# Row statistics of the second token pair taken in the first pair's chunks and kept, and all due times set anew, in a two-layer attention and SwiGLU kernel

## The chip, the cores and the metric

The kernel runs on one core of a Trainium2 chip. The metric is the device time of one execution in microseconds (us). A core has five engines that run side by side: TensorE (PE in the profile, with PEld for its weight loads), VectorE (DVE), ScalarE (ACT), GpSimd (POOL) and SyncE (SP), which here issues nearly all DMAs. Each engine takes its own instructions strictly in the order in which they were written into the program, and waits on semaphores where an instruction needs another engine's result.

## What is computed

Two layers, each of which is an attention block A and a feed-forward block B on x of 2048 tokens by 512 features, in float32. Both layers share the weights.

```python
x = x + A(layernorm(x)); x = x + B(layernorm(x))      # layer 0
x = x + A(layernorm(x)); x = x + B(layernorm(x))      # layer 1

def layernorm(x):
    m = mean(x, axis=-1); v = var(x, axis=-1)
    return (x - m) / sqrt(v + 1e-5)

def A(x):                          # 32 heads of 16, 4 segments of 512 tokens, one after the other
    for each segment s:
        p = softmax(q_s k_s^T / 4 + causal mask);  a_dot = p v_s
        a_mem = (phi(q_s) M) / (phi(q_s) z + 1e-6)
        o_s = g * a_mem + (1 - g) * a_dot
        M += phi(k_s)^T v_s;  z += sum(phi(k_s))
    return o @ wo

def B(x):                          # 512 -> 1792 -> 512
    return (silu(x @ w_gate) * (x @ w_up)) @ w_down
```

## The kernel before

**Precision.** A float32 operand is split into a high part of type float32r and the rest, also float32r; a product is made of three TensorE passes (high by high, rest by high, high by rest). So every weight and every activation that goes into a matmul is first copied by ACT (the high part) and then subtracted by DVE or POOL (the rest).

**Attention.** There are 32 units for a layer: 4 segments by 4 groups of 8 heads by 2 halves. Of each unit there are projections (`qk_proj`, `v_proj`, through `mm3`, line 295), row maxima (`mx_units`, lines 558 and 564), scores, exponentials and products with v (`at_units`, lines 609 to 636), the memory (`mem_read`, `mem_update`) and, a segment later, `wo_proj`. A segment's rows are loaded and normalised in `ln_pre` and transposed in `ln_fin`. Each projection's result goes through DRAM (`scrq`, `scrk`) and comes back as `cq` and `ck`.

**Feed-forward.** The tokens are taken in four blocks of 512, as two pairs: blocks 0 and 1 (m = 0), then 2 and 3 (m = 1). The 1792 hidden features are taken in seven chunks of 256. Chunk 0 of a pair is computed plainly (`up`, line 1019). Chunks 1 to 6 use Strassen's scheme with 7 products instead of 8 on the halves of the 2x2 block matrix (`strassen`, lines 1049, 1062, 1064). For them `make_t` (lines 963, 984, 985) builds the sums and differences of a pair's transposed rows on DVE, 28 DVE operations a pair, and `load_s` (lines 902 to 916) those of the weights on POOL. `finish` (lines 1003 to 1006) multiplies gate and up and splits the product; `down` (lines 1093, 1098) multiplies a chunk with w_down and adds it to the rows of the block, and with the last chunk stores them. The opening of the feed-forward part is interleaved with the last units of attention by `hook` and `EARLY_AT`.

**Normalising in the feed-forward part.** `ln(b)` loads each of a block's four tiles of 128 rows from `xmid` into `xin` (two buffers, in turn), and calls `ln_norm`: `bn_stats` (line 367) and `bn_aggr` (368) on DVE, the addition of epsilon (369) and the power of -1/2 (370) on POOL, the product of mean and scale on DVE (372), and the normalising itself on POOL (379) into `xn` (two buffers, in turn). `ln_transpose` brings the tile onto TensorE (387), and ACT (391) and DVE (392) copy and split it.

**What sets the order.** The program is written as a list of operations, each with an engine, a planned cost, what it reads and writes, and a due time, `P.prio`. `at(v)` sets the due time to `base + v * T`, with T = 15.0 in attention and 16.7 in the feed-forward part. `Program.issue` is a list scheduler: it goes through time with the planned costs, and on each engine takes among the operations that are ready the one with the smallest due time; an engine never idles in the plan while something is ready. The resulting order of each engine is what is written into the program. So a due time decides only between operations that are ready together, and buffers (which are reused in program order) hold operations back besides. The due times come from tables: `OFF` (attention, one row for each layer: `at` scores, `mx` maxima, `lf` transposes, `lp` normalising, `mr`/`mu` memory, `wo`, `qk`, `qe`, `v` projections), `PRE` (start of a layer: `w1` to `w3`, `lv`, `lo` weight loads, `gate` the gate, `c` and `mb` clearings, `v`, `dv`, `qk1` projections), `EP` (opening of the feed-forward part) and the constants `PAIR` (between the pairs), `STEP` (between the chunks), `TAT` (`make_t`, for each pair), `WAT` (the first `load_s`), `FIN` (`finish`) and `WQ1`. A planned cost on POOL is the first argument of `gp`.

The lines that set the due times of the feed-forward loop, in the form before:

```python
v = m * PAIR                          # the pair
...
at(v + WAT);     load_s(1, "g")
at(v + TAT[m]);  make_t(m)
...
v = m * PAIR + 2 + (c - 1) * STEP     # chunk c = 1..6
at(v);           gs = strassen(c, "g", m)
...
at(v + FIN);     finish(...)
```

## Time and profile before

| what | value |
|---|---|
| median of 3 runs | 1877.89 us (1874.88 to 1881.86) |
| the profiled execution | 1875.12 us |
| its span, first to last instruction | 1873.4 us |
| mean granted TensorE clock | 0.996 |
| instructions | 33021 |

All views below are of that one execution. In the rows of stages the columns are: from and to in us, length, then for PE, PEld, DVE, ACT and POOL the busy time with the number of instructions, and last the mean granted TensorE clock, the mean busy share of the DMA engines and GB/s. In the rows of groups stand line, engine, operation, what it writes and reads, the shapes and the number of instructions, then busy time and mean duration in ns, then the idle time before them and what ended it. In the rows of waits stand the waiting engine, tile and line, what it waited for, the total in us, the number of waits and the longest. In the rows of the timeline stand start and length in us; a wait before the instruction stands in brackets with what ended it. A name such as `s` or `ps` stands for all buffers of that kind.

### The profile page before, as it was taken

The numbers are of one execution on the slowest core, as the hardware profiler recorded it, in microseconds if no ns is written. First come the engines' busy times: TensorE is split into PE (matmuls) and PEld (weight loads), VectorE is DVE, ScalarE is ACT, GpSimd is POOL, SyncE is SP. The second block draws the span as 40 slices with busy tenths as digits, with TensorE's granted clock in tenths as the row PEclk, the third lists the DMA queues.
The fourth block names the chain that finished last, engine by engine and source line by source line (L and its number), as shares of the span: only waits on it lengthen the run. The fifth ranks groups of instructions, "written<-read, shape, count | busy, mean of one in ns | idle before, by whom it ended". The sixth has DMA issues, their size and how long they took to land.

```text
span 1873.4 us, 33021 instructions
## 1 busy us (share of the span) xinstructions
PE 1823.4 (97%) x11360; PEld 1449.7 (77%) x11360; DVE 1406.8 (75%) x3834; ACT 872.0 (47%) x1629; POOL 916.9 (49%) x1184
## 2 busy tenths in 40 slices
PE   7999999999999999999989999999999999999999
PEld 5787787777778887788777777788777778878887
DVE  6878788788876678765776777787898766795656
ACT  4565564555533433333435655556454433333432
POOL 6344444444656554646533444444445647444551
PEclk9999999999999999999999999999999999999999
DMA  8435444464232132212363353455542311221111
GB/s 243 142 103 146 137 130 148 145 198 132 77 120 62 46 90 85 62 45 63 118 209 103 103 162 111 136 169 138 191 121 74 124 51 57 86 78 51 44 58 45
DMA packets 126967, 206.14 MB, mean 110 GB/s; under 512 B 14160, under 2 KB 52048, under 8 KB 126800
## 3 DMA queue, kind: packets, MB, share of 16 engines
q1 hardware_dynamic: 124752, 203.49, 36.5%
q8 instruction: 91, 1.49, 0.3%
q10 hardware_dynamic: 2048, 0.53, 0.1%
q14 instruction: 76, 0.62, 0.1%
HBM read 136.34 MB, written 67.11 MB: 109 GB/s over the span
## 4 chain that ended last, share of the span: by engine, by line
PE 74%; DVE 14%; issue 5%; DMA 4%; ACT 2%; POOL 2%; SPq 1%; DVEq 0%; POOLq 0%; ACTq 0%
PE ps L1049 23%; PE ps L295 14%; PE ps L1093 13%; PE ps L558 6%; PE ps L636 6%; PE ps L609 6%; DVE junk L564 3%; PE ps L1019 2%; DMA ck<-scrk 2%; DVE tt L963 1%; DVE s L1098 1%; DVE s L985 1%; PE ps L387 1%; DMA s<-nm 1%; DVE mx L564 1%
## 5 line engine op out<-in xcount | busy, mean ns | idle before, releaser
L1049 PE MATMUL ps<-s,s 128*128 128x512 f32 x2016 | 547.2, 396 | 7.7 <-DVE s L985 4.6
L295 PE MATMUL ps<-s,s 128*128 128x512 f32 x1536 | 524.0, 406 | 4.7 <-ACT s L451 3.0
L564 DVE CUSTOM_DVE_ANT_0 junk<-ps,amask 128x128 bf16<-128x128 f32 (+3 forms) x1024 | 433.7, 484 | 48.8 <-PE ps L558 47.4
L1049 PEld LDWEIGHTS ps<-s,s 128*128 128x128 f32 x2016 | 376.4, 188 | 103.4 <-DVE s L985 5.5
L1093 PE MATMUL ps<-s,vt 128*128 128x512 f32 x1296 | 379.9, 398 | 2.2 <-ACT vt L1005 2.2
L295 PEld LDWEIGHTS ps<-s,s 128*128 128x128 f32 x1536 | 286.1, 190 | 53.2 <-issue 5.6
L615 ACT ACTIVATE s<-ps 128x512 f32<-128x512 f32 x448 | 253.8, 610 | 106.8 <-PE ps L609 95.8
L1093 PEld LDWEIGHTS ps<-s,vt 128*128 128x128 f32 x1296 | 245.8, 190 | 59.0 <-ACT vt L1005 2.6
L558 PE MATMUL ps<-ck,s 127*128 127x256 f32 (+2 forms) x1024 | 277.7, 335 | 7.2 <-DMA ck<-scrk 5.9
L609 PE MATMUL ps<-s,ck 128*128 128x256 f32 x1280 | 249.9, 287 | 4.8 <-DMA s<-nm 2.9
L609 PEld LDWEIGHTS ps<-s,ck 128*128 128x128 f32 x1280 | 220.9, 189 | 36.2 <-DVE mx L564 4.3
L1098 DVE TENSOR_TENSOR s<-s,ps 128x512 f32<-128x512 f32 x224 | 150.0, 682 | 91.6 <-PE ps L1093 91.5
L619 POOL TENSOR_SCALAR_AFFINE_SELECT s<-s 128x512 f32<-128x512 f32 x192 | 126.4, 661 | 170.2 <-ACT s L615 167.8
L558 PEld LDWEIGHTS ps<-ck,s 127*128 127x128 f32 x1024 | 178.2, 190 | 31.7 <-issue 6.0
L492 POOL TENSOR_SCALAR s<-raw 128x512 fp32r<-128x512 f32 x64 | 45.2, 706 | 177.2 <-ACT raw L491 168.8
L916 POOL TENSOR_TENSOR s<-mem,s 128x512 fp32r<-128x512 f32 x96 | 130.3, 1357 | 0.0
L1019 PE MATMUL ps<-s,s 128*128 128x512 f32 x384 | 124.0, 400 | 0.9 <-ACT s L391 0.9
L923 POOL COPY turn<-vt 128x1 f32<-128x1 f32 x20 | 3.7, 184 | 232.9 <-DVE vt L1006 232.9
L636 PE MATMUL ps<-s,vt 128*32 128x384 f32 (+3 forms) x1536 | 115.7, 419 | 0.2 <-DVE mx L564 0.2
L636 PEld LDWEIGHTS ps<-s,vt 128*32 128x32 f32 x1536 | 43.4, 109 | 64.2 <-issue 46.5
L615 ACT ACTIVATE pc<-ps 128x512 f32<-128x512 f32 x128 | 78.9, 616 | 20.5 <-PE ps L609 19.8
L1019 PEld LDWEIGHTS ps<-s,s 128*128 128x128 f32 x384 | 71.6, 188 | 19.3 <-ACT s L391 1.9
(171 smaller groups left out, 2589.0 us busy)
## 6 DMA issues: line engine op xcount, KB each, us to landing
s<-scrq SPq DMA_DIRECT2D x128, 192.0 KB, 3.5
ck<-scrk SPq DMA_DIRECT2D x128, 192.0 KB, 4.4
scrq<-s SPq DMA_DIRECT2D x32, 512.0 KB, 3.6
scrk<-s SPq DMA_DIRECT2D x32, 512.0 KB, 3.3
scrq<-s SPq DMA_DIRECT2D x32, 256.0 KB, 3.2
scrk<-s SPq DMA_DIRECT2D x32, 256.0 KB, 2.5
s<-xmid SPq DMA_DIRECT2D x32, 256.0 KB, 5.3
xin<-xmid SPq DMA_DIRECT2D x32, 256.0 KB, 2.6
```

The source lines that it names most:

```text
L295: pe(n, passes, lambda: nc.tensor.matmul(view(ps.ap), lhsT=av(a.ap), rhs=bv(b.ap), start=start, stop=stop), [(a, rk[0]), (b, rk[1])], [ps])
L558: nc.tensor.matmul(ps.ap[:, a * 256:a * 256 + nk], lhsT=cq.ap[0:127, 2 * j + p, qt * 128:(qt + 1) * 128], rhs=ck.ap[0:127, p, 0:nk], start ...
L564: dve(w, lambda a=a, qt=qt, w=w, ps=ps, junk=junks[qt % 2]: nc.vector.tensor_tensor_reduce(out=junk.ap[:, :w], in0=ps.ap[:, a * 256:a * 25 ...
L609: nc.tensor.matmul(ps.ap[:, 256 * p:256 * p + 256], lhsT=ck.ap[:, p, kt * 128:kt * 128 + 128], rhs=cq.ap.rearrange("r (j p) c -> r p j c", ...
L615: act(512, lambda: nc.scalar.activation(view().rearrange("p x i c -> p (x i c)"), ps.ap, AF.Exp, scale=SCALE), [ps], [(Pb, key)], table="exp")
L619: gp(0.593, lambda: nc.gpsimd.affine_select(out=view()[:, 0], in_=view()[:, 0], pattern=[[0, 4], [1, 128]], compare_op=OP.is_ge, fill=0.0, ...
L636: nc.tensor.matmul(ps.ap[32 * i:32 * i + 32, qt * 128:(qt + k) * 128], lhsT=vt.ap[:, kt, VW * hd:VW * hd + 32], rhs=view(k=k)[:, :, idx], ...
L916: gp(n / 400, lambda hi=hi, lo=lo, src=src: nc.gpsimd.tensor_sub(lo(), src(), hi().bitcast(F32)), [read, (wt, (o0, 0))], [(wt, (o0, 1))])
L1019: pe(512, 1, lambda i=i, j=j, kc=kc, x=x, ps=ps, wt=wt: nc.tensor.matmul(ps.ap, lhsT=wt.ap[:, i, kc, cs], rhs=XT[b][j].ap[:, :, kc], start ...
L1049: pe(512, 1, lambda i=i, kc=kc, x=x, buf=buf, view=view: nc.tensor.matmul(ps.ap, lhsT=w.ap[:, o, i, kc], rhs=view(buf.ap, kc), start=(x == 0),
L1093: pe(512, 1, lambda i=i, j=j, fi=fi, x=x, ps=ps, wt=wt, cs=cs: nc.tensor.matmul(ps.ap, lhsT=ht.ap[:, 0:2048].rearrange("p (f a c) -> p f a ...
L1098: dve(512, lambda ps=ps, t=t: nc.vector.tensor_add(xb.ap[:, t, :], xb.ap[:, t, :], ps.ap), [ps, (xb, t)], [(xb, t)])
```

## The change

It has three parts.

1. `ln_norm` is taken apart: `ln_stats` holds lines 367 to 372, and `ln_norm` calls it only when it isn't handed finished statistics. A new function `stats(b)` loads the four tiles of a block and keeps their two columns of statistics in a new buffer `rsall`. It is called for block 2 in chunk 3 and for block 3 in chunk 4 of pair 0, with the due time of the chunk plus 1.0. `ln(2)` and `ln(3)` load the rows again and only normalise.
2. All due times in the tables are new.
3. The planned costs of POOL's operations are new.

```diff
+STC, STV = 3, 1.0
-PAIR, STEP, WAT, TAT = 11.852, 7.441, 15.217, (16.363, 16.627)
+PAIR, STEP, WAT, TAT = 14.368, 2.101, 18.234, (6.403, -7.127)
-FIN = 4.95
-WQ1 = -11.849
+FIN = -18.907
+WQ1 = -35.921
-OFF = ({'qe': (-8.094, 0.816), 'at': (3.287, 3.306), 'mx': (-0.131, -0.724), 'lf': (1.377, -12.744), 'mr': (-1.477, 8.495), 'mu': (-0.96, 1.713), 'wo': (1.48, 1.471), 'qk': (-3.167, 5.871), 'v': (3.082, -3.254), 'lp': (-0.438, 1.332)},
-       {'qe': (-13.863, -20.735), 'at': (1.287, 1.907), 'mx': (0.952, -1.245), 'lf': (-8.163, -17.558), 'mr': (12.428, -6.81), 'mu': (-3.524, 1.251), 'wo': (0.699, 4.133), 'qk': (2.417, 0.184), 'v': (-2.402, 1.541), 'lp': (-15.902, 3.529)})
-PRE = {'w1': -7.923, 'w2': -0.782, 'w3': 1.908, 'c': -7.288, 'mb': 12.995, 'lv': 2.037, 'lo': 1.091, 'gate': 1.265, 'v': 1.734, 'dv': 17.818, 'qk1': -29.691, 'mx': -0.352}
-EP = {'w': 7.501, 'wn': 13.81, 'ln': -3.176, 'dn': -0.03, 'up': -1.79}
+OFF = ({'qe': (-12.069, -0.112), 'at': (3.013, 4.323), 'mx': (-0.349, -1.509), 'lf': (-11.355, -18.547), 'mr': (5.356, 2.737), 'mu': (-0.143, 0.695), 'wo': (1.6, 0.626), 'qk': (-2.074, 4.084), 'v': (4.063, -4.114), 'lp': (-0.398, 0.122)},
+       {'qe': (-5.653, -33.367), 'at': (0.791, 0.725), 'mx': (0.972, -0.361), 'lf': (-24.563, -10.349), 'mr': (10.993, -6.845), 'mu': (-3.987, -0.752), 'wo': (5.165, -12.31), 'qk': (-0.437, 1.019), 'v': (-0.149, 1.562), 'lp': (-34.686, 18.305)})
+PRE = {'w1': -22.172, 'w2': 0.92, 'w3': 0.959, 'c': 10.734, 'mb': 21.744, 'lv': 1.211, 'lo': 1.157, 'gate': -12.416, 'v': 41.354, 'dv': 19.399, 'qk1': -33.145, 'mx': -6.145}
+EP = {'w': 27.342, 'wn': 3.181, 'ln': -1.549, 'dn': 3.109, 'up': -0.862}
...
-    def ln_norm(xt, view, xk, tags, on_act=False):
-        st, mv, rs = sb("bst", [128, 6], ring=4), sb("bmv", [128, 2], ring=4), sb("brs", [128, 2], ring=4)
+    def ln_stats(xt, view, xk, home=None):
+        st, mv = sb("bst", [128, 6], ring=4), sb("bmv", [128, 2], ring=4)
+        rs, i = rk = home or (sb("brs", [128, 2], ring=4), 0)
         dve(512, lambda: nc.vector.bn_stats(out=st.ap, in_=view(xt.ap)), [(xt, xk)], [st])
         dve(8, lambda: nc.vector.bn_aggr(out=mv.ap, in_=st.ap), [st], [mv])
         gp(0.18, lambda: nc.gpsimd.tensor_scalar_add(mv.ap[:, 1:2], mv.ap[:, 1:2], EPS), [mv], [mv])
...
+        return rk
+
+    def ln_norm(xt, view, xk, tags, on_act=False, rk=None):
+        rs, i = rk = rk or ln_stats(xt, view, xk)
         xn = sb(tags, [128, 512])
...
+        RS = {}
+        two_rs = sb("rsall", [128, 16])
+
+        def stats(b):
+            for t in range(4):
+                xt = sb("xin", [128, 512], ring=2)
+                load_rows(xt, x_in, b * 512 + t * 128)
+                RS[b, t] = ln_stats(xt, lambda a: a, None, (two_rs, 8 * b + 2 * t - 16))
+
         def ln(b):
...
-                ln_transpose(ln_norm(xt, lambda a: a, None, XN2), XT[b][0], XT[b][1], t)
+                ln_transpose(ln_norm(xt, lambda a: a, None, XN2, rk=RS.get((b, t))), XT[b][0], XT[b][1], t)
...
             for c in range(1, NF):
                 v = m * PAIR + 2 + (c - 1) * STEP
+                if m == 0 and c in (STC, STC + 1):
+                    at(v + STV)
+                    stats(c + 2 - STC)
                 at(v)
                 gs = strassen(c, "g", m)
```

The planned costs on POOL (us): the power in `ln_stats` 0.46 to 0.6, normalising 0.75 to 0.85, `qk_proj` 0.59 to 0.70 and 1.23 to 1.32, the mask on the exponentials 0.593 to 0.66, the rest of `of` 1.23 to 1.32, the sums in `load_s` 0.65 to 0.85, and its splits from n / 400 to 0.3 + n / 480.

30 lines of the change are left out of this document (15 added, 15 removed).

## The prediction

> **What bounds the kernel now.** I read the busy table first, then the engines by stage, then the waits of PE, and last the timeline at the places where PE waits.
>
> ```profile
> span 1873.4 us, 33021 instructions
> PE 1823.4 (97%) x11360; PEld 1449.7 (77%) x11360; DVE 1406.8 (75%) x3834; ACT 872.0 (47%) x1629; POOL 916.9 (49%) x1184
> ```
>
> PE is busy for 1823.4 of 1873.4 us. The change removes no matmul, so what it can win is mainly within the 50.0 us in which PE stands idle. The execution took 1875.1 us, 1.7 more than its span, and the median of the runs is 1877.9, another 2.8 more: I work out a difference against the profiled execution and set it on the median.
>
> Engines by stage (attention of layer 0, opening of its feed-forward part, chunks of pair 0, turn from pair 0 to pair 1, boundary of the layers, and the same in layer 1):
>
> ```profile
> 0.00:60.00 60.00, 43.63 (x199) 34.70 (x200) 40.61 (x137) 28.11 (x51) 32.03 (x55) 0.97 0.72 220
> 60.00:470.00 410.00, 404.20 (x3403) 319.69 (x3402) 326.39 (x1254) 229.94 (x455) 178.72 (x271) 1.00 0.48 142
> 470.00:545.00 75.00, 72.92 (x388) 56.08 (x387) 62.52 (x109) 33.30 (x60) 46.34 (x54) 1.00 0.36 113
> 545.00:690.00 145.00, 145.00 (x626) 116.66 (x625) 98.68 (x151) 58.58 (x102) 81.35 (x89) 1.00 0.19 54
> 690.00:770.00 80.00, 76.82 (x345) 61.08 (x343) 68.39 (x113) 28.80 (x52) 43.36 (x48) 1.00 0.31 97
> 935.00:1000.00 65.00, 58.87 (x299) 46.64 (x298) 45.71 (x159) 26.24 (x48) 22.02 (x21) 0.95 0.54 174
> 1000.00:1400.00 400.00, 392.10 (x3313) 310.50 (x3312) 313.71 (x1203) 224.86 (x442) 172.13 (x265) 1.00 0.49 141
> 1400.00:1475.00 75.00, 72.97 (x388) 56.07 (x387) 61.61 (x107) 33.37 (x60) 46.04 (x54) 1.00 0.35 112
> 1625.00:1690.00 65.00, 62.29 (x278) 49.89 (x277) 55.78 (x88) 23.58 (x44) 34.97 (x36) 0.97 0.27 86
> ```
>
> Length less PE busy gives the idle time: start 16.4, attention 5.8 and 7.9, openings 2.1 and 2.0, turns 3.2 and 2.7, boundary 6.1; in the chunks nothing. What ended it, from the waits of PE:
>
> ```profile
> PE ps L387 <- ACT xn L376: 9.9, 1, 9.9
> PE ps L558 <- DMA ck<-scrk: 5.9, 5, 2.2
> PE ps L1049 <- DVE s L985: 4.6, 2, 2.3
> PE ps L295 <- ACT s L451: 3.0, 2, 1.8
> ```
>
> The first is the ramp at the start. The third is the pair of turns: PE waits for the last split of `make_t`.
>
> **The change, part by part.** *The turn.* The statistics of a block's four tiles in the opening (470 to 545) and in the turn (690 to 735), then DVE's and PE's timeline:
>
> ```profile
> L367 DVE BATCH_NORM_STATS2 bst<-xin x8: 649/680/689, 470.7 to 500.9; 128x6 f32<-128x512 f32 x8
> ```
> ```profile
> L367 DVE BATCH_NORM_STATS2 bst<-xin x4: 655/670/685, 702.4 to 712.7; 128x6 f32<-128x512 f32 x4
> ```
> ```profile
> 706.09 0.16 DVE L372 SCALAR_TENSOR_TENSOR brs<-bmv,brs 128x1 f32<-128x1 f32 x1 [2.01 <-POOL brs L370]
> ...
> 726.58 1.28 DVE L963 TENSOR_TENSOR xn<-s 128x512 f32<-128x512 f32 x2
> ...
> 743.52 1.68 DVE L963 TENSOR_TENSOR of<-of,s 128x512 f32<-128x512 f32 x1
> ...
> 752.59 1.21 DVE L985 TENSOR_TENSOR s<-tt,s 128x512 fp32r<-128x512 f32 x1
> ```
> ```profile
> 752.73 0.50 PE L1049 MATMUL ps<-s,s 128*128 128x512 f32 x1 [2.32 <-DVE s L985]
> ```
> ```profile
> 726.58:753.80 27.22, 27.12 (x40) 1.00 0.18 57
> ```
> ```profile
> 726.60:753.80 27.20, 14.79 (x20) 1.00 0.18 57
> ```
> ```profile
> 726.60:753.80 27.20, 6.86 (x8) 1.00 0.18 57
> ```
>
> The last three rows are DVE from the first operation of `make_t` to its last: all of it, `L963` alone, `L985` alone. It is full, and `make_t` is (14.79+6.86)/28 = 0.77 us an operation. So the turn ends when DVE has done its pile, and PE pays 2.3 us. What one tile's statistics cost:
>
> ```profile
> L367 DVE BATCH_NORM_STATS2 bst<-xin 128x6 f32<-128x512 f32 x60 | 40.4, 680 | 7.5 <-DMA xin<-in_A_x_dram 6.1 <-DMA xin<-xlay 1.5
> L368 DVE BATCH_NORM_AGGREGATE bmv<-bst 128x2 f32<-128x6 f32 x64 | 10.8, 172 | 0.6
> L369 POOL TENSOR_SCALAR bmv<-bmv 128x1 f32<-128x1 f32 x64 | 17.8, 281 | 41.5 <-DVE bmv L368 39.9 <-DVE rm L694 0.9 <-DVE brs L372 0.3
> L370 POOL TENSOR_TENSOR brs<-bmv,mhalf 128x1 f32<-128x1 f32 x64 | 38.8, 609 | 3.7
> L372 DVE SCALAR_TENSOR_TENSOR brs<-bmv,brs 128x1 f32<-128x1 f32 x64 | 16.3, 255 | 18.7 <-POOL brs L370 18.4
> ```
>
> On DVE 0.68+0.17+0.26 = 1.11 us, and as a chain through POOL 2.0 us. A turn holds four tiles, those of block 3; the opening's eight are those of blocks 1 and 2, so block 2 is measured there already. By 4 x 1.11, 4.4 us leave a full DVE, and 2.0 us go between a row's landing and its normalising (at 706.09 DVE itself waits 2.0 for POOL). That is more than the 2.3 us of PE's wait. Besides, `make_t` of pair 1 gets a smaller due time (7.24 instead of 28.48 units of 16.7), so its operations go ahead of the adds of `down`. I take the two waits (4.6) and 0.4 of the small ones behind them: -5.0. Bounds: -5.9 (all idle of both turns) and 0.
>
> Waits have a second price:
>
> ```profile
> 935.00:952.00 17.00, 12.66 (x48) 9.57 (x47) 11.43 (x19) 6.44 (x10) 6.63 (x3) 0.90 0.68 204
> 952.00:962.00 10.00, 10.00 (x44) 8.38 (x45) 8.61 (x34) 1.73 (x3) 1.92 (x2) 0.83 0.65 241
> 1680.00:1690.00 10.00, 7.73 (x28) 5.90 (x27) 6.78 (x9) 2.33 (x5) 6.10 (x6) 0.83 0.27 79
> ```
>
> The granted clock is 0.83 over the 10 us around the wait of layer 1's turn, so 0.17x10 = 1.7 us more are lost; the same in each of the two boundary stretches. In layer 0's turn the clock stayed at 1.00 (row 690:770). So -1.7 for one turn; bounds 0 and -3.4. The Trainium skill ("TensorE: Matmul & The Clock Gate", What's actually happening) says that the clock halves after at least one idle window of about 3.4 us. The waits here are 2.3 us, shorter than that, and three of them are followed by a low clock: the trace differs, and the row decides; by the rule alone the clock terms would be nothing and my sum 3.4 us smaller.
>
> *The statistics in their new place.* The list scheduler starts the most urgent ready operation, and where none is ready, a less urgent one. The statistics need only rows in `xmid` and a free `xin`, so I expect them as soon as block 1's tiles are out, about 490 to 545, ahead of chunk 3. There are eight tiles in each opening instead of four: 4 x 1.11 = 4.4 us of DVE into 75 - 62.5 = 12.5 us of idle. `make_t` of pair 0 is now due at 6.40, ahead of them (7.20, 9.30), where it stood behind block 2 (16.36 against 10.65). I take 0; bounds -2.0 per opening (its idle) and +4.4 (all on the chain). If they stand in the chunks, DVE idles 46 us of 145 there.
>
> *Rows twice.* 16 more loads of 256 KB:
>
> ```profile
> xin<-xmid SPq DMA_DIRECT2D x32, 256.0 KB, 2.6
> ```
> ```profile
> SPq L860 <- POOL s L916: 115.6, 19, 15.9
> ```
>
> The DMA engines are at 0.19 to 0.36 in those stages, so bandwidth costs nothing. But SP takes its queue in order: in chunks of pair 0 it stood 115.6 of 145 us before weight loads whose `raw` POOL had not freed. A row load behind such a wait keeps `bn_stats` waiting at DVE's head, and behind it the adds that free Strassen's banks. 0 while the loads lie in the opening; one such stall could be some us.
>
> *Boundary.* The elementwise end of a chunk (`FIN`) goes from +4.95 to -18.9, ahead of everything on ACT and DVE. Now:
>
> ```profile
> 937.74 7.16 PE L1093 MATMUL ps<-s,vt 128*128 128x512 f32 x23 [2.18 <-ACT vt L1005]
> ...
> 951.91 0.48 PE L558 MATMUL ps<-ck,s 127*128 127x256 f32 x2 [2.16 <-DMA ck<-scrk]
> ```
>
> The first wait is for that end's cast. When it goes, the second comes late: the ck chain starts elsewhere. I take -1.0 net and one clock window, -1.7; bounds -9.5 (6.1 idle and two windows) and 0.
>
> *Start.* `make_gate`'s five loads move ahead of the rows of x:
>
> ```profile
> 10.23 2.45 SPq L341 DMA_DIRECT2D bet<-in_A_beta_dram  x4
> ```
>
> About 2.5 us of SP ahead of what ends the ramp of 9.9; against that, the last wq and wk loads, now behind the gate, move up, and PE waits 3.0 for `L451`. 0; bounds -3.0 and +2.5.
>
> *Attention.* Only due times move, and the planner's POOL prices:
>
> ```profile
> L902 POOL TENSOR_TENSOR mem<-phiq 128x256 f32<-128x256 f32 x24 | 19.2, 802 | 6.5 <-DMA phiq<-in_B_w_gate_dram 6.4
> ```
>
> It planned 0.65 for this and measured 0.80; `L370` 0.46 against 0.61; the new prices (0.85, 0.60) lie within 6%. A plan that knows POOL makes fewer waits that it did not see. Of 13.7 us idle in both attentions I take a fifth, -2.6. Two orders of the same work differ there by 2.1 us today. Bounds -13.7 and as much the other way.
>
> Sum: -5.0 - 1.7 + 0 + 0 - 2.7 + 0 - 2.6 = -12.0. On the profiled execution 1863.1; on the median 1865.9.
>
> **The rivals.** *Only the turn moves* (waits in the boundary and attention change place): -6.7, 1871.2, within 0.5%. For it: those waits sit on DMA chains, which no due time shortens. *POOL meets the earlier make_t*: at 743.52 above an operation took 1.68, next to 0.64 at 726.58. Were POOL busy all along, `make_t` would take 28 x 1.0 us longer, by its busy share in the turn (43.4 of 80) 15. The 4.4 us taken off and the earlier start only cover that, the turns win nothing, and -5.3 is left: 1872.6. The Trainium skill ("SBUF — State Buffer", two separate sides) states such a lock between DVE with two SBUF inputs and GpSimd; the row agrees.
>
> *It doesn't do what it says*: the statistics crowd the opening instead of the chunks: +8.8 in both, -12.0 + 8.8 = -3.2, 1874.7.
>
> *Slower: make_t holds DVE.* What PE needs for a matmul, from the chain of waits:
>
> ```profile
> 571.42 13.21 PE ps L1049 x57
> ```
>
> With `make_t` first, the adds of `down` (three `pj` banks) and the end of `up` queue behind its 28 operations. PE can run meanwhile three groups of `down` and the 96 matmuls of `up`, at 13.21/57 = 0.232 each 4.2 + 22.3 = 26.5 us. That covers 28 operations up to a mean of 0.95 us; at 1.2 the block lasts 33.6, and PE stands 7.1 us per turn: +14.2 against today, 1892. Against it: the mean is 0.77 today, and the scheduler lets others in while a split waits for ACT.
>
> **How the numbers follow.** A measurement of this kernel can tell about 0.5%, 9.4 us. Chances: forecast 0.48; only the turn, or POOL meets make_t, 0.22; crowded opening 0.13; slower 0.17. So faster 0.48, same 0.35, slower 0.17. Range: all lower bounds together would be far (-5.9-3.4-4.0-9.5-3.0-13.7); I give two thirds, 1852. Above, 1889 takes in all but the far end of the slower rival.
>
> **What would show it.** Right: no `L367` between 690 and 715, `make_t` beginning before 722, no wait for `L985` over 0.5 us, clock 1.00 in layer 1's turn, the wait for `L1005` gone. Wrong: PE waiting for `L1098` or `L1003` in the turns, `L963` means over 0.95, `L367` waiting for `xin` in the chunks, or attention's idle above 13.7.

## The result: slower by 1%, and the profile after

| | before | after |
|---|---|---|
| median of 4 runs | 1876.78 us (1874.88 to 1881.86) | 1897.24 us (1893.69 to 1898.97) |
| the profiled execution | 1875.12 us | 1898.97 us |
| its span | 1873.4 us | 1897.2 us |

The ratio is 1.0102, with a 95% interval of 1.0077 to 1.0128. The forecast was 1865.9 us with a range up to 1889; the time lies above it. A line of the kernel from 28 on stands 1 to 18 further down after the change: `bn_stats` is L369, the transposes L393, `make_t` L978, L999 and L1000, Strassen's products L1064, `finish` L1018 to L1021, `down` L1108 and L1113, `ln_norm` on ACT L382 and on POOL L385.

The busy table of the page, after:

```profile
span 1897.2 us, 33002 instructions
PE 1829.6 (96%) x11360; PEld 1448.7 (76%) x11360; DVE 1397.2 (74%) x3834; ACT 858.7 (45%) x1625; POOL 903.0 (48%) x1184
```

PE does the same 11360 matmuls, so the time went where PE stood idle or ran slowly. The engines by stage, after (columns as before):

```profile
0.00:60.00 60.00, 37.29 (x157) 29.25 (x158) 34.43 (x111) 22.67 (x40) 31.14 (x50) 0.94 0.66 200
60.00:475.00 415.00, 406.19 (x3374) 321.16 (x3373) 323.85 (x1258) 230.71 (x455) 173.19 (x264) 1.00 0.50 142
475.00:565.00 90.00, 84.10 (x460) 63.89 (x460) 71.28 (x149) 39.02 (x72) 54.06 (x76) 0.96 0.37 121
565.00:710.00 145.00, 143.57 (x616) 114.57 (x615) 96.43 (x146) 55.05 (x98) 80.28 (x88) 1.00 0.19 54
710.00:790.00 80.00, 79.34 (x359) 64.13 (x358) 66.38 (x106) 29.57 (x54) 37.55 (x42) 1.00 0.32 102
955.00:1020.00 65.00, 59.91 (x309) 46.43 (x308) 48.78 (x165) 25.93 (x48) 20.16 (x22) 1.00 0.60 187
1020.00:1410.00 390.00, 382.96 (x3239) 304.32 (x3237) 301.00 (x1169) 215.77 (x437) 169.03 (x257) 1.00 0.51 143
1410.00:1505.00 95.00, 86.92 (x479) 65.66 (x479) 74.13 (x160) 37.76 (x71) 52.93 (x73) 1.00 0.38 117
1650.00:1710.00 60.00, 58.71 (x268) 46.98 (x267) 53.86 (x78) 25.49 (x47) 28.07 (x27) 1.00 0.28 89
```

Length less PE busy is now 22.7 us at the start (16.4 before), 5.9 and 8.1 in the openings (2.1 and 2.0), 0.7 and 1.3 in the turns (3.2 and 2.7), 5.1 at the boundary (6.1). The windows are set to the stages of this execution, so their lengths differ from those of before. To compare whole stages I summed a typical duration for each matmul in the order in which they start, as a measure of work done, and took at equal work the time of after less that of before, between borders that lie at 9.9, 74.9, 452, 566, 681, 776, 916, 965, 1362, 1503, 1614, 1714 and 1864 us of before. That is a reckoning of mine from the traces; it is of one execution each, which lies up to 4 us from its median. What it can tell is seen where two traces have the same order on TensorE: e16 below and before up to 1414 us, e1 below and after from 60 us on, e5 below and after up to 474 us, e11 below and before outside the turns. There the chunks agree within 0.4 us and the turns within 1.1, while a start, an attention, an opening or the boundary still differs by up to 3. Between attention and opening of layer 1, and between the start and attention of layer 0, the plans mix the matmuls differently, and the border moves with the way a matmul is weighed: by the recorded lengths of the matmuls, after loses 6.8 us in layer 1's opening and wins 0.1 in its attention. The sum of the two stays the same within 1 us. "Lost" in this table is us against before:

```
                    ramp  start  att0  open0  chunks  turn0  chunks  bound  att1  open1  chunks  turn1  tail   all
after                6.1    1.8   4.5    7.9     1.5   -3.3     1.9   -2.5  -3.3    9.8     1.0   -2.8   1.4  23.9
```

So the turns won about what they should, and the ramp, the start and the two openings together lost 25.6 us. The boundary's -2.5 can't be put down to the change: e11, whose order there is that of before, shows -2.4. The waits of PE, after:

```profile
PE ps L393 <- ACT xn L382: 16.0, 1, 16.0
PE ps L1064 <- ACT s L999: 5.3, 5, 1.3
PE ps L712 <- DVE brs L374: 4.8, 1, 4.8
...
PE ps L1108 <- ACT vt L1020: 3.6, 3, 1.6
```

The first is the ramp, 9.9 us before. The wait for `make_t`'s last split (4.6 us before) is not among them. The second and most of the rest are small waits, many of them in the openings.

**The start.** SyncE's timeline after, then all engines (start and length in us), then the summary of the DMA engines over the first 20 us in 40 slices of 0.5 us, after and before:

```profile
1.82 1.92 SPq L342 DMA_DIRECT2D bet<-in_A_beta_dram  x4
3.79 0.43 SPq L348 DMA_DIRECT2D ginv<-in_A_beta_dram  x1
4.26 0.91 SPq L363 DMA_DIRECT2D tt<-in_A_x_dram  x2
```
```profile
12.29 0.21 ACT L345 ACTIVATE gnot<-bet 128x8 f32<-128x8 f32 x1 [6.92 <-DMA bet<-in_A_beta_dram]
...
13.00 0.69 DVE L369 BATCH_NORM_STATS2 bst<-tt 128x6 f32<-128x512 f32 x1
...
16.00 3.99 PE L393 MATMUL ps<-ident,xn 128*128 128x128 f32 x16 [16.00 <-ACT xn L382]
```
```profile
DMA  0000199910000000025788934999999998998889
GB/s 0 0 0 1 53 306 344 319 28 1 1 1 1 0 0 5 9 53 215 275 298 308 156 113 170 357 361 362 309 310 298 296 265 241 320 322 270 201 294 328
```
```profile
DMA  0000799998899999999999999984100000002999
GB/s 0 0 0 25 223 303 309 246 119 250 311 385 381 348 304 342 350 316 297 290 297 320 347 377 385 389 288 100 42 1 1 1 1 1 5 14 63 289 340 367
```

The five loads of the gate cost SP only 1.92 + 0.43 = 2.35 us of issuing. But while they are under way, the queue moves almost nothing: 28 GB/s and less from 4.0 to 8.5 us, though the rows of x have been issued at 4.26. By the trace's records of packets, those that start from 4.5 to 7.5 us are all of 4 and 8 bytes, 30 to 60 in 0.5 us, where some 300 of 512 bytes started in 0.5 us before; in the kernel each of the four `bet` loads is 128 runs of 8 bytes. In before the same hole stands at 14 to 18.5 us, where PE has other work. The first rows are issued 2.4 us later than in before and take 8.8 us to land instead of 4.9, so that `bn_stats` starts at 13.00 and the first transpose at 16.00 instead of 9.9.

**The turn.** `make_t` of pair 1 in layer 0, as three answers on DVE (all, L978, L1000), and the engines in the same stretch, after and before:

```profile
738.77:758.84 20.07, 20.04 (x35) 1.00 0.14 47
```
```profile
738.77:758.84 20.07, 12.97 (x20) 1.00 0.14 47
```
```profile
738.77:758.84 20.07, 5.49 (x8) 1.00 0.14 47
```
```profile
738.77:758.84 20.07, 20.07 (x88) 16.15 (x87) 20.04 (x35) 6.76 (x12) 0.00 (x0) 1.00 0.14 47
```
```profile
726.58:753.80 27.22, 24.90 (x108) 19.87 (x107) 27.12 (x40) 9.54 (x17) 13.44 (x9) 1.00 0.18 57
```

It takes 20.1 us instead of 27.2, (12.97+5.49)/28 = 0.66 us an operation instead of 0.77, PE is busy throughout, and POOL, 13.44 us busy beside `make_t` before, does nothing there.

**The opening.** Statistics of blocks 2 and 3 in layer 0 (source view of L369, 502 to 560 us), and two of PE's waits from its timeline:

```profile
L369 DVE BATCH_NORM_STATS2 bst<-xin x9: 659/684/689, 503.9 to 549.2; 128x6 f32<-128x512 f32 x9
```
```profile
491.04 0.92 PE L393 MATMUL ps<-ident,xn 128*128 128x128 f32 x4 [1.15 <-POOL xn L385]
...
522.12 0.79 PE L1064 MATMUL ps<-s,s 128*128 128x512 f32 x1 [1.21 <-ACT s L999]
```

One of the nine is the last tile of block 1; the other eight are the moved ones, and they lie in the opening, not in chunks 3 and 4 (after 565). The waits are short and for several producers. The clock is 0.96 there, 0.04 x 90 = 3.6 us more; but in e1, which has the same order and the same waits in this opening, it stayed at 1.00, so that this part is of the execution and not of the plan.

### The profile page after: what moved, and what is told of

The parts are those of the page before. It is cut to its first block, busy times and chain, and to the rows that moved or that the text cites. A ratio compares the mean times of both kernels' runs of the same rounds, so it can differ in the third digit from the quotient of the medians.

```text
span 1897.2 us, 33002 instructions
## 1 busy us (share of the span) xinstructions
PE 1829.6 (96%) x11360; PEld 1448.7 (76%) x11360; DVE 1397.2 (74%) x3834; ACT 858.7 (45%) x1625; POOL 903.0 (48%) x1184
## 4 chain that ended last, share of the span: by engine, by line
PE 79%; DVE 10%; issue 4%; ACT 2%; DMA 2%; POOL 1%; SPq 0%; DVEq 0%; ACTq 0%; POOLq 0%
PE ps L1064 22%; PE ps L296 16%; PE ps L1108 15%; PE ps L564 7%; PE ps L642 6%; PE ps L615 6%; PE ps L1034 4%; DVE junk L570 2%; PE ps L393 1%; DVE vt L1021 1%; DMA s<-nm 1%; DMA ck<-scrk 1%; PE ps L696 1%; DVE mx L570 1%; DVE xn L1077 1%
## 5 line engine op out<-in xcount | busy, mean ns | idle before, releaser
L1064 PE MATMUL ps<-s,s 128*128 128x512 f32 x2016 | 550.1, 397 | 12.6 <-ACT s L999 5.3
L1064 PEld LDWEIGHTS ps<-s,s 128*128 128x128 f32 x2016 | 376.0, 188 | 114.2 <-DVE tt L1077 10.5
L1108 PE MATMUL ps<-s,vt 128*128 128x512 f32 x1296 | 378.1, 395 | 4.1 <-ACT vt L1020 3.6
L296 PEld LDWEIGHTS ps<-s,s 128*128 128x128 f32 x1536 | 286.6, 190 | 51.9 <-issue 5.4
L1108 PEld LDWEIGHTS ps<-s,vt 128*128 128x128 f32 x1296 | 243.6, 188 | 61.5 <-ACT vt L1020 5.1
L615 PEld LDWEIGHTS ps<-s,ck 128*128 128x128 f32 x1280 | 215.5, 189 | 37.7 <-issue 4.4
L1113 DVE TENSOR_TENSOR s<-s,ps 128x512 f32<-128x512 f32 x224 | 152.4, 685 | 113.4 <-PE ps L1108 113.0
L922 POOL TENSOR_TENSOR s<-mem,s 128x512 fp32r<-128x512 f32 x96 | 125.9, 1312 | 0.7 <-ACT s L921 0.7
L497 ACT COPY raw<-ps 128x512 f32<-128x512 f32 x64 | 38.0, 593 | 144.6 <-PE ps L296 95.9
```

The lines of the kernel that those rows point to most:

```text
L296: pe(n, passes, lambda: nc.tensor.matmul(view(ps.ap), lhsT=av(a.ap), rhs=bv(b.ap), start=start, stop=stop), [(a, rk[0]), (b, rk[1])], [ps])
L615: nc.tensor.matmul(ps.ap[:, 256 * p:256 * p + 256], lhsT=ck.ap[:, p, kt * 128:kt * 128 + 128], rhs=cq.ap.rearrange("r (j p) c -> r p j c", ...
L922: gp(0.3 + n / 480, lambda hi=hi, lo=lo, src=src: nc.gpsimd.tensor_sub(lo(), src(), hi().bitcast(F32)), [read, (wt, (o0, 0))], [(wt, (o0, ...
L1064: pe(512, 1, lambda i=i, kc=kc, x=x, buf=buf, view=view: nc.tensor.matmul(ps.ap, lhsT=w.ap[:, o, i, kc], rhs=view(buf.ap, kc), start=(x == 0),
L1108: pe(512, 1, lambda i=i, j=j, fi=fi, x=x, ps=ps, wt=wt, cs=cs: nc.tensor.matmul(ps.ap, lhsT=ht.ap[:, 0:2048].rearrange("p (f a c) -> p f a ...
L1113: dve(512, lambda ps=ps, t=t: nc.vector.tensor_add(xb.ap[:, t, :], xb.ap[:, t, :], ps.ap), [ps, (xb, t)], [(xb, t)])
```

## The experiments

My theory after the result was: the gate's loads cost the ramp, the statistics crowd the openings, the rest of the loss lies in the new due times. The rivals: that the statistics cost nothing where they are and single due times of the opening do the harm; that the prices do; and, last, that any other order loses in the openings. No kernel below leaves any of the computation out. Five sets ran beside the kernel before, whose median was 1876.32 (e1 to e4), 1875.81 (e5 to e8), 1875.65 (e9 to e11), 1877.40 (e12 to e15) and 1875.50 us (e16 to e18). What each lost by stage:

```
                    ramp  start  att0  open0  chunks  turn0  chunks  bound  att1  open1  chunks  turn1  tail   all
e1_gate_back        -0.3   -1.5   2.0    6.2     1.4   -3.3     2.0   -2.9  -3.9   10.5     0.9   -3.9   1.4   8.6
e2_no_stats          6.1    0.1   3.4    4.0     1.2   -1.8     1.9   -2.6   0.1    8.5     1.1    0.1   1.5  23.5
e3_stats_only       -0.4   -0.1   0.8    7.6     0.6    2.8    -0.1   -2.3  -1.9    9.5    -0.3    5.9  -0.0  22.0
e4_pool_prices       0.2   -0.5   9.8    3.7     1.5    4.2     2.0   -1.8   6.3   11.0     1.2    3.7  -0.0  41.1
e5_opening_back      5.7   -1.3   3.9    6.6     1.4   -3.3     2.0   -2.9  -1.9    7.5     1.0   -3.9   1.5  16.1
e6_ln_due            5.0    1.3   3.3    9.2     1.5   -3.4     2.0   -2.7  -2.3   16.4     1.0   -2.9   1.5  30.0
e7_in_chunks        -0.6    0.9   2.8    4.4    -0.2   -3.3     1.9   -2.7  -3.7    8.3    -0.1   -3.8   1.3   5.5
e8_before_in_chunks -0.4    1.0  -0.3   -0.6    -0.1    6.2    -0.1   -1.1   1.6    0.6    -0.4    6.8  -0.1  13.0
e9                  -0.4   -0.1   2.2    4.0    -0.2   -3.4     2.0   -2.4  -4.5    8.9     0.3   -3.9   1.3   3.8
e10_before_turn     -0.4   -0.4   0.3   -0.6    -0.1    3.6     0.7   -2.0  -2.5    9.0    -0.1    3.4   0.3  11.1
e11_turn_alone      -0.1    1.3  -1.4    0.8     0.1   -0.7     0.2   -2.4  -0.4   -0.6    -0.4   -1.2  -0.0  -4.7
e12_old_prices       4.9    3.5   5.9   13.5    -0.0   -4.1     0.3    0.5   1.1   15.7     0.1   -4.5   0.5  37.3
e13                 -1.1    1.6   5.4    5.9     0.6   -3.7     0.3    4.4  -0.2   12.5     0.2   -4.2   0.3  22.1
e14                 -0.1    2.8   1.9    5.2     0.5   -3.3     2.0   -2.3   8.1    7.6    -0.3   -3.9   1.2  19.4
e15                  0.1    0.9   2.3    2.5    -0.1    5.2     0.6   -1.3  -0.3   10.1    -0.2    2.6   0.1  22.5
e16                 -0.4   -0.6   2.1    2.4     0.0    0.8    -0.0   -1.2  -1.2    3.1    -0.1    0.1  -0.0   5.1
e17                 -0.4    0.9   4.2    5.8     0.1   -3.3     1.9   -2.7  -0.9   17.2     0.3   -3.9   1.3  20.6
e18                 -0.1   -0.4   0.5    3.1     0.5    0.7     0.7   -1.7  -2.5   12.5    -0.5   -1.5  -0.0  11.3
```

**e1: the gate's due time back.** From the changed kernel:

```diff
-'gate': -12.416
+'gate': 1.265
```

> The changed kernel with one number set back: the due time of make_gate (-12.416 to 1.265), so its five small loads go behind the rows of x again. Theory (the gate's loads hold up the DMA queue): the first transpose starts at about 10 us instead of 16.0, and the time falls by 6 to 9 us, to about 1889. Rival (the start is late for the other due times of the start, or what is won there is lost in the waits behind it): the first transpose moves but the time falls by under 3 us.

1887.48 us (6 runs), ratio 1.0054 [1.0038, 1.0071]: 9.8 us of the 20.5 come back. PE's first wait and the DMA summary over the first 20 us in e1:

```profile
PE ps L393 <- ACT xn L382: 9.7, 1, 9.7
```
```profile
DMA  0000199968799999999999999999999999998200
GB/s 0 0 0 1 54 323 344 327 98 139 283 352 344 406 374 345 334 323 309 296 292 289 290 291 292 317 337 382 389 377 389 393 393 393 377 389 212 39 1 1
```

The hole is gone from 4 to 8.5 us (another begins at 18.5, where the gate's loads now are), and with it the longer ramp. Of the changed plans, those that keep the early gate lose 4.9 to 6.1 us in the ramp, those with the gate back nothing. From 60 us on, the order of e1 is that of after on every engine, so the 9.8 us are the gate's: 6.4 in the ramp and 3.3 in the start, where PE's wait of 4.8 us at L712 became one of 2.0. This part is shown. The other 10.7 us of after's loss stand in what comes behind.

**e2: no separate statistics.**

```diff
-                    stats(c + 2 - STC)
+                    pass
```

> The changed kernel without the calls of stats, so that blocks 2 and 3 are measured in ln again and their rows loaded once; all due times and prices as in the changed kernel. Theory A (the statistics crowd the openings of the feed-forward parts): PE's idle time in the openings falls from 5.9 and 8.1 to about 2 each, and the time by 10 us or more, less the 2 to 4 that the turns won: about 1886 to 1889. Rival B (the due times of the openings make the loss): the openings stay, the turns lose 2 to 5 us each, and the time rises to about 1900.

1898.67 us, 1.0107 [1.0084, 1.0131]: the same as after. The openings still lose 4.0 and 8.5 us without the moved statistics, and the turns win less (-1.8 and +0.1 instead of -3.3 and -2.8). By this run the statistics' leaving is worth 1.5 to 2.9 us a turn, and most of the openings' loss, 12.5 of 17.7 us, is not theirs.

**e3: the new structure alone**, with every due time and price of before.

```diff
-PAIR, STEP, WAT, TAT = 14.368, 2.101, 18.234, (6.403, -7.127)
+PAIR, STEP, WAT, TAT = 11.852, 7.441, 15.217, (16.363, 16.627)
...
-        gp(0.6, lambda: nc.gpsimd.tensor_tensor(out=rs.ap[:, i:i + 1], ...
+        gp(0.46, lambda: nc.gpsimd.tensor_tensor(out=rs.ap[:, i:i + 1], ...
```

> The kernel before with the statistics taken and kept (the new functions, called in chunks 3 and 4), and all due times and POOL prices of before. Theory A (crowding): the openings lose 5 us or more each, the turns win up to 3 each, the time is 1880 to 1890. Rival B (due times): the statistics alone are worth what the turns win, 1871 to 1876.

1896.65 us, 1.0103 [1.0084, 1.0122]. Neither expectation came: it is the same total as after, in other places: openings +7.6 and +9.5, and the turns, which the statistics have left, are longer by 2.8 and 5.9.

**e4: the new POOL prices alone**, in the kernel before.

```diff
-        gp(0.75, lambda: nc.gpsimd.tensor_scalar(out=xn.ap, ...
+        gp(0.85, lambda: nc.gpsimd.tensor_scalar(out=xn.ap, ...
```

and the other POOL prices likewise.

> The kernel before with the new planned costs of POOL's operations alone. If the prices make better plans, as the prediction's attention term had it: 1870 to 1875, attention's idle below 13.7 us. Rival (the due times of before fit the old prices, and any new plan from them is as likely worse): 1880 or more.

1916.93 us, 1.0219 [1.0192, 1.0245], the slowest of all, with 9.8 and 6.3 us lost in attention. This plan with prices nearer to the measured durations is worse.

**e5 and e6: due times of the opening.** e5 takes `EP`, `WAT` and the first `TAT` of before, e6 only one entry of `EP`:

```diff
-PAIR, STEP, WAT, TAT = 14.368, 2.101, 18.234, (6.403, -7.127)
+PAIR, STEP, WAT, TAT = 14.368, 2.101, 15.217, (16.363, -7.127)
-EP = {'w': 27.342, 'wn': 3.181, 'ln': -1.549, 'dn': 3.109, 'up': -0.862}
+EP = {'w': 7.501, 'wn': 13.81, 'ln': -3.176, 'dn': -0.03, 'up': -1.79}
```
```diff
-EP = {'w': 27.342, 'wn': 3.181, 'ln': -1.549, ...
+EP = {'w': 27.342, 'wn': 3.181, 'ln': -3.176, ...
```

> The changed kernel with the due times of the feed-forward opening set back (EP, WAT and make_t of pair 0). Theory (the openings are late because their work is due later: block 1's rows are normalised and transposed too late, and make_t after them): make_t of pair 0 begins before attention's last unit is out, as in the kernel before, the openings' loss against before (7.9 and 9.8 us of the same TensorE work) falls to 4 or less each, what the statistics cost there, and the time to 1885 to 1890. Rival (the openings' loss is the statistics alone, or that of any plan with these prices): it stays within 3 us of the changed kernel.

> The changed kernel with a single number set back, the due time of ln in the opening (-1.549 to -3.176, 27 us earlier). Theory (this number alone makes block 1 late): half or more of the openings' loss goes, 1885 to 1892. Rival (it is the set of due times together): under 3 us.

e5 1891.33 us, 1.0089 [1.0074, 1.0104]; e6 1904.28 us, 1.0148 [1.0126, 1.0171]. On TensorE e5's order differs from after's only about the openings (474 to 610 and 1397 to 1575 us of after), and its median is 5.9 us lower; the table gives the openings 1.3 and 2.3 us of that, no more than two executions of one order can differ by there. e6 is worse than after. The due times of the opening alone don't bring its loss back.

**e7 and e8: statistics held in the chunks.** A due time did not put them there; a dependency does. Each row load waits until the first half of block 1's product of the chunk before has been split, the work of its `finish`. e7 is e1 with this, e8 is e3 with this.

```diff
-        def stats(b):
+        def stats(b, hold):
...
                 load_rows(xt, x_in, b * 512 + t * 128)
+                P.ops[-1].deps |= set(hold)
...
-                    stats(c + 2 - STC)
+                    stats(c + 2 - STC, [hts[1].w[0, 1]])
```

> The changed kernel with make_gate's due time set back, and with the row loads of stats held until the chunk before is finished, so that the statistics really stand in chunks 3 and 4. Theory (crowding): no statistics of blocks 2 and 3 in the openings, their loss falls by 2 to 5 us each against the kernel with the gate alone set back, the chunks stay full, and the time is 1878 to 1884. Rival (the statistics hurt nowhere in the opening, its due times do): as with the gate alone, 1885 to 1890. Third: a row load behind SP's waits holds up VectorE in the chunks, which then lose PE time: above 1890.

> The kernel before with the statistics held in chunks 3 and 4 by the same wait, all due times and prices of before. Theory (the statistics in the chunks cost nothing and shorten the turns): openings as before or better, turns up to 3 us shorter each, 1868 to 1876. Rival (any new plan from due times that were not set for it is worse): 1885 or more, with turns or openings longer.

e7 1881.54 us (6 runs), 1.0030 [1.0017, 1.0044]; e8 1887.91 us, 1.0074 [1.0057, 1.0091]. The source view of L369 and the engines in the chunks and the turn in e7, then the turn and the stretch of `make_t` in e8:

```profile
L369 DVE BATCH_NORM_STATS2 bst<-xin x8: 660/686/689, 597.6 to 637.8; 128x6 f32<-128x512 f32 x8
```
```profile
560.00:690.00 130.00, 130.00 (x561) 104.49 (x560) 89.16 (x152) 48.64 (x87) 83.02 (x103) 1.00 0.25 77
690.00:775.00 85.00, 84.35 (x381) 68.25 (x380) 71.59 (x114) 32.34 (x58) 40.97 (x46) 1.00 0.32 101
```
```profile
690.00:775.00 85.00, 77.71 (x339) 61.43 (x338) 65.99 (x100) 28.82 (x52) 40.62 (x42) 0.98 0.29 90
```
```profile
726.10:756.90 30.80, 25.80 (x108) 19.69 (x106) 30.73 (x42) 10.65 (x19) 15.26 (x13) 1.00 0.18 61
```

The statistics and the additional loads of the rows stand in the chunks without any idle time of PE (130.00 of 130.00): there they are free. In e8 they have left the openings (-0.6 and +0.6) and the turns, yet the turns are longer than in before by 6.2 and 6.8 us: `make_t` still starts at 726.1 and takes 30.8 us, with POOL 15.26 us busy beside it. So the statistics were not what held the turn. The due times matter more: e10 below draws `make_t` forward and wins 2.6 and 3.4 us on this, e11 below draws it forward in the kernel before and shortens it to 22.0 us with the statistics still in the turn, and e15, which sets the chunks' back, loses 5.2 and 2.6 us in the turns where e9 won 3.4 and 3.9.

**e9 and e10.** e9 is e7 with the three changes of e5. e10 is e8 with the due time of pair 1's `make_t` drawn forward:

```diff
-PAIR, STEP, WAT, TAT = 11.852, 7.441, 15.217, (16.363, 16.627)
+PAIR, STEP, WAT, TAT = 11.852, 7.441, 15.217, (16.363, -4.611)
```

> The changed kernel with three things set right together: make_gate's due time back, the statistics held in chunks 3 and 4, and the due times of the feed-forward opening (EP, WAT, make_t of pair 0) back. Theory (the openings' loss is the crowd of statistics and the late due times together): the openings' loss goes from 4.4 and 8.3 us (statistics held) to 2 or less each, the turns keep their gain of 3 to 4 each, and the time is 1866 to 1873. Rival (attention's new due times or the new prices make the openings late, whatever EP says): the openings keep 4 us or more each, 1878 to 1884.

> The kernel before with the statistics held in chunks 3 and 4, and make_t of pair 1 due as early as in the changed kernel (7.24 units instead of 28.48); all other due times and prices of before. Theory (the turn is won by make_t's due time, and the statistics' leaving helps only with it): make_t takes 20 us instead of 31 (27 before), the turns go from +6.2 and +6.8 us against before to -2 or less, and the time is 1866 to 1873. Rival (it takes the whole new set): turns stay at +4 or more, 1882 or more.

e9 1880.64 us (12 runs), 1.0027 [1.0015, 1.0039]; e10 1888.87 us, 1.0071 [1.0054, 1.0087]. e10's turns are 2.6 and 3.4 us better than e8's, between what the two expectations said: `make_t` of layer 0 takes 25.5 us, with POOL 12.7 us busy beside it. But layer 1's opening, whose own due times were not touched, went from +0.6 to +9.0, and its attention from +1.6 to -2.5: together 4.3 us lost. The edit changed TensorE's order not only in the turn, but all the way from 734 to 1537 us of e8, layer 1's attention and opening with it.

**e11: the earlier make_t alone**, the edit of e10 in the kernel before.

> The kernel before with the due time of make_t of pair 1 alone (28.48 to 7.24 units), no statistics kept. If the due time alone wins the turn: make_t 20 to 22 us, both waits for its last split gone, 1870 to 1874. If the statistics have to leave too: within 2 us of before or slower.

1873.56 us (12 runs), 0.9989 [0.9977, 1.0001]: the best of all, and not told from before. `make_t` takes 22.0 us in both layers, with POOL 7.0 us busy beside it, and the turns win 0.7 and 1.2 us. The openings hold (+0.8 and -0.6), although this is the edit of e10: here it changed TensorE's order only in the turns (742 to 815 and 1672 to 1695 us of before), so the openings are those of before. In the waits of e11 that for the last split is gone, and another has come in its place:

```profile
PE ps L1049 <- DVE tt L1062: 3.4, 2, 1.7
```

**e12 to e15: single groups back.** e12 is after with the POOL prices of before, e13 the same in e9, e14 is e9 with `OFF` of before, e15 is e9 with the chunks' due times of before:

```diff
-        gp(0.85, lambda: nc.gpsimd.tensor_scalar(out=xn.ap, ...
+        gp(0.75, lambda: nc.gpsimd.tensor_scalar(out=xn.ap, ...
```
```diff
-OFF = ({'qe': (-12.069, -0.112), ...
+OFF = ({'qe': (-8.094, 0.816), ...
```
```diff
-PAIR, STEP, WAT, TAT = 14.368, 2.101, 15.217, (16.363, -7.127)
-FIN = -18.907
-WQ1 = -35.921
+PAIR, STEP, WAT, TAT = 11.852, 7.441, 15.217, (16.363, -4.611)
+FIN = 4.95
+WQ1 = -11.849
```

> The changed kernel with the planned costs of POOL of before. If the new prices cost the openings: their loss falls by 3 us or more each, 1885 to 1890. If the new due times were set with the new prices and need them: 1900 or more. If prices matter little to this plan: within 4 us of the changed kernel's 1897.

> The kernel with the three mendings (gate, statistics held, opening's due times) and the planned costs of POOL of before. If the prices are what is left of the openings' loss: it goes from 4.0 and 8.9 us to 2 or less each, 1868 to 1873. If not: 1878 or more.

> The kernel with the three mendings and the due times of attention (OFF) of before. If attention's new due times are what is left of the openings' loss: 2 us or less each, while attention itself gives back the 2 to 4 us that layer 1 won: 1870 to 1878. If not: openings at 4 us or more, 1880 or more.

> The kernel with the three mendings and the due times of the chunks (PAIR, STEP, FIN, WQ1) of before, make_t of pair 1 still due at 7.24 units. If the chunks' due times are what is left of the openings' loss: 2 us or less each, 1868 to 1876; the turns then show whether they were won by make_t's due time or by the chunks'. If not: openings as in e9, 1880 or more.

| run | median, us | ratio to before, 95% |
|---|---|---|
| e12 | 1913.42 | 1.0201 [1.0180, 1.0222] |
| e13 | 1895.61 | 1.0103 [1.0082, 1.0125] |
| e14 | 1893.72 | 1.0095 [1.0074, 1.0115] |
| e15 | 1897.83 | 1.0114 [1.0089, 1.0139] |

No group set back restores the openings (2.5 to 13.5 and 7.6 to 15.7 us lost), and each loses 13 to 17 us in all against the kernel that it was made from. e12 and e4 are mirror images: old prices with new due times lose, new prices with old due times lose.

**e16, e18 and e17: a nudge of 10 ns.** That left the question whether these runs measure the edited values at all, or only that the order is another. One planned cost, of normalising a tile on POOL, was moved by 10 ns: in the kernel before up (e16) and down (e18), in e7 up (e17).

```diff
-        gp(0.75, lambda: nc.gpsimd.tensor_scalar(out=xn.ap, ...
+        gp(0.76, lambda: nc.gpsimd.tensor_scalar(out=xn.ap, ...
```

> The kernel before with one planned cost moved by 10 ns: normalising a tile on POOL 0.75 to 0.76 us (the trace has 0.82). The operations, their due times and the buffers are those of before; only the order that the list scheduler writes out is another. Theory A (a fitted plan: the due times were fitted to one exact plan, and any nudge gives another plan, which is nearly always longer): 1880 to 1900 us, with the loss spread over stages that the nudged operation has nothing to do with, openings among them. Theory B (prices and due times act smoothly, so that the 22 to 40 us of the earlier runs with other prices measure those prices): within 3 us of before, 1873 to 1880, since 60 tiles by 10 ns are 0.6 us of POOL.

> The kernel before with the same planned cost moved by 10 ns the other way, 0.75 to 0.74 us. Theory A (a fitted plan): 1880 to 1900 us, with another distribution over the stages than the nudge up. Theory B (smooth): within 3 us of before, 1873 to 1880, and on the other side of it than the nudge up.

> The changed kernel with the gate set back and the statistics held in the chunks (1881.5 us), with the same planned cost moved by 10 ns, 0.85 to 0.86 us. Theory A (a fitted plan): the openings' losses of 4.4 and 8.3 us change by several us, and the whole by 3 to 20 us, mostly up. Theory B (smooth; the openings' losses belong to the due times as they stand): openings stay at 4 to 5 and 8 to 9, the whole at 1879 to 1885.

| run | median, us | ratio to before, 95% |
|---|---|---|
| e16, before, 0.75 to 0.76 | 1879.25 (10 runs) | 1.0018 [1.0006, 1.0031] |
| e18, before, 0.75 to 0.74 | 1887.84 (4 runs) | 1.0070 [1.0048, 1.0091] |
| e17, e7, 0.85 to 0.86 | 1894.46 (4 runs) | 1.0100 [1.0083, 1.0117] |

Both directions lose: 3.7 and 12.3 us on before, and 12.9 us on e7. e16's median lies at the upper edge of what the smooth theory gave, though its interval lies above 1; e18 and e17 are plainly the first theory's, and a smooth effect would not lose both ways. Operations, due times and buffers are the same in these kernels, only the order differs. How much of it differs is not the same: on TensorE, e16 leaves before's order only at 1414 us, in layer 1's opening (171 positions of 11360), e18 in layer 0's opening at 499 us and up to the end of layer 1's at 1550 us (2729 positions), e17 that of e7 in layer 0's opening and from 1264 us to the end of layer 1's. So up to there nothing of e16 is the nudge's: its 2.1 and 2.4 us in layer 0 are of the execution, and the +3.1 in layer 1's opening is no more than such differences. e18 lost 3.1 and 12.5 us in the openings, e17 5.8 and 17.2 where e7 had 4.4 and 8.3 (by the recorded lengths, layer 1's are 9.3, and 12.0 where e7 had 5.3), while the chunks stay within 0.7 us and the turns within 1.5 us of the kernel that was nudged. What PE waited longest for in layer 1's opening, in e18 and in e17:

```profile
PE ps L387 <- POOL xn L379: 5.8, 4, 3.7
```
```profile
PE ps L579 <- DVE mx L570: 3.6, 1, 3.6
```

Two nudged plans, two different waits. The openings are the stage in which the last units of attention are interleaved with the first work of the feed-forward part, and PE idled only 2.1 and 2.0 us there in the kernel before. Of the other 19 plans, e11 has before's order in layer 1's opening; of the 18 with another order there, e8 holds it to within 1 us, e16 loses 3.1 us, and the other 16 lose 7.5 us or more (3.3 or more by the recorded lengths).

## Why the prediction was wrong

**The start (0, bounds -3.0 to +2.5).** This term was mis-sized, and it is the largest single one that an experiment isolates: set back, it returned 9.8 us. I priced the gate's loads by SP's time to issue them, 2.45 us. The queue time is the price, some 4.5 us in which nearly no bytes arrive and behind which the rows land: the first transpose came 6.1 us later, and a wait of 4.8 us and a clock of 0.50 followed in the start. The hole stood in the trace of before, between 14 and 18.5 us.

**The statistics in their new place (0, bounds -2.0 to +4.4 an opening).** That they would lie in the opening was right (503.9 to 549.2 us, no L369 in the chunks), and that they would be free in the chunks too (e7). But the openings lost 7.9 and 9.8 us, more than the bound. The failed step is the bound itself: it counted the DVE time of four tiles and took the rest of the opening as given. A new plan reorders all of it. From e3 to e8 the openings recover 8.2 and 8.9 us when the statistics are held back, from e1 to e7 only 1.8 and 2.2, which is within what two executions of one order can differ by, and e2 without them still loses 4.0 and 8.5. Since a nudge of 10 ns (e18) costs layer 1's opening some 9 to 12.5 us, none of these differences can be put down to crowding alone. That layer 1's opening loses clear of this noise in 16 of 18 other orders is shown; which operation in which order makes the difference is open, and so is how much of after's loss the statistics themselves make.

**The turn (-5.0 and -1.7).** Right in kind and near in size: -3.3 and -2.8 at equal work, the wait for L1000 gone from the turns, no L369 in the turn before 760, the clock 1.00 in layer 1. `make_t` began at 738.8; without the 21.8 us that had been lost by then that is 717.0, before 722 as forecast. The reason was half wrong. I credited 4.4 us of statistics; e8 lost 6.2 and 6.8 us in the turns without any statistics in them, and e2 won 1.8 in one with them. What shortened `make_t` was the new order, which left POOL nothing to do beside it: 28 x (0.77-0.66) = 3.1 us from the operations, and 35 DVE operations in the stretch instead of 40. The other plans bear this out: in layer 0's turn `make_t` takes 20.1 us in all ten plans that have the chunks' new due times and the statistics out of the turn (POOL at most 0.4 us busy there), 22.0 with 7.0 us of POOL (e11), 25.5 with 12.7 (e10), 27.2 with 13.4 (before), 30.8 with 15.3 (e8). In e2 POOL is 7.3 us busy and `make_t` still takes 20.1: there it is POOL that is held, one operation of 128x256 for 4.95 us. *POOL meets the earlier make_t* named the mechanism and had its sign wrong for this plan; for e10 it has it right. That two-input DVE work and POOL delay one another, as the Trainium skill says ("SBUF — State Buffer", two separate sides), agrees with these rows (0.66 us with POOL at 0.00, 0.77 with POOL at 13.44).

**The boundary (-1.0 and -1.7).** -2.5 measured, PE's idle time 5.1 us where it was 6.1, clock 1.00 where it was 0.95; the wait for L1020 is still there, 1.6 us at most. That the sum is near is in part luck: e11, with before's order and before's three long waits there (2.2, 2.8 and 1.8 us), also has a clock of 1.00 and -2.4. The low clock that I priced was that of one execution.

**Attention (-2.6).** Measured +4.5 and -3.3, together +1.2. The failed step is that a plan with better POOL prices makes fewer unseen waits: alone they cost 16.1 us in attention (e4). e17's 10 ns alone moved layer 1's attention by +2.8 us against e7. (A fifth of 13.7 is 2.7, not 2.6; that changes nothing.)

**Rows loaded twice (0).** Right: the page shows 48 loads of `xin` from `xmid` instead of 32, and in e7 the chunks that hold them have no idle time.

**The slower rival** (`make_t` holds DVE above 0.95 us an operation) did not come; its mean fell to 0.66. What made the kernel slower was no mechanism on my list. I summed terms for operations that I could see move, and all other waits of the new order entered as zero. Besides the gate's loads, it is the openings' loss that stands in that zero.

## What to carry to other kernels

When a change sets the due times of a whole list-scheduled program anew, nudge the plan first (one price by 10 ns) and see how far the time moves: here 4 to 13 us, so a difference of that size between two plans says little about the edited values. Compare the engines' orders in the two traces as well: what a stage differs by though its order is the same is the noise of a stage, here up to 3 us. A due time only ranks what is ready; where an operation must not start early, a dependency holds it. A DMA that is drawn ahead of others is to be priced by how long the queue's bytes stop, read from the slices around the same loads in their old place, and not by its issue.

## What was not expected of the hardware

Five loads of 1.0 to 16 KB let the queue's rate fall from over 300 to about 1 GB/s for some 4 us, in both kernels and in two places, with loads of 256 KB issued behind them. The packets of that time are of 4 and 8 bytes, 30 to 60 in 0.5 us.

The clock falls after short waits, too. Stretches of 5 us in the opening of after, and at the start around PE's wait of 4.8 us:

```profile
490.00:495.00 5.00, 3.96 (x17) 3.50 (x17) 4.20 (x10) 3.66 (x8) 4.75 (x10) 0.66 0.23 65
...
520.00:525.00 5.00, 3.79 (x11) 2.68 (x11) 5.00 (x11) 1.23 (x2) 0.79 (x2) 0.70 0.01 3
```
```profile
35.00:40.00 5.00, 4.61 (x13) 3.87 (x14) 0.47 (x3) 0.58 (x1) 2.33 (x4) 0.50 0.90 246
```

The waits of 1.15 and 1.21 us shown above stand in the first two: the granted clock there is 0.66 and 0.70. So a small wait in the opening can cost PE more than its length, while others of 1.0 to 1.5 us (turns, boundary) left it at 1.00. It is not the wait alone: e1 has the same order there and waits of 1.16 and 1.21 us at the same two places, and its clock stayed at 1.00.

A run of DVE operations with two SBUF inputs can hold a POOL operation for several of its own. At the start of after, DVE's and POOL's timelines:

```profile
21.25 8.51 DVE L458 TENSOR_TENSOR s<-s,s 128x512 fp32r<-128x512 f32 x14
```
```profile
25.86 4.38 POOL L498 TENSOR_SCALAR s<-raw 128x512 fp32r<-128x512 f32 x1 [1.51 <-ACT raw L497]
```

The POOL operation, 0.69 us in the mean, took 4.38 us, until 0.5 us after the 14 operations of DVE had ended.
